# Sixty of 2048 exponential tiles move from ScalarE to VectorE

## The chip, the cores and the metric

The kernel runs on one core of a Trainium2 chip. The core has engines with queues of their own that work at the same time: TensorE (PE, matrix products into PSUM), ScalarE (ACT, functions of one tensor), VectorE (DVE, element by element work), GpSimd (POOL) and SyncE (SP, which starts most DMA transfers here). An engine takes its queue in order; engines wait for each other by semaphores. The metric is device microseconds from start to end of one execution; less is better.

## The reference, cut to what matters

Two branches read the same `x` of 2048 rows and 512 columns. Branch A is attention with 32 heads of 16 dimensions; branch B is a state space convolution. A sigmoid gate mixes them.

```python
q, k, v = heads(x @ wqkv)                    # 32 heads, 2048 rows, 16 columns
p = softmax(einsum("bhqd,bhkd->bhqk", q, k) * 16 ** -0.5)
a = concat(einsum("bhqk,bhkd->bhqd", p, v)) @ wo
K = einsum("dn,dnl,dn->dl", Cc, exp(dt * A * l), dt * Bc).real
b = causal_convolution(x, K) + x * Dskip     # by FFT in the reference
g = sigmoid((x * gate_w).sum(-1))
out = g * a + (1 - g) * b
```

The softmax needs 32 x 2048 x 2048 exponentials. On 128 partitions that is 2048 tiles of 128x512.

## The kernel before, in words

**Tiles.** A block is 512 query rows by four heads, and there are 32 blocks (`NQ` = 512 quads are 32 blocks x 16 key tiles). A quad is four tiles of 128 keys x 512 queries, one for each of the four heads of the block. Four heads lie on the 32-row strips of the array, and a mask (`Qm`, L669) selects which of the two heads in a strip is meant.

**The main loop** (L1366 to L1380) walks over 683 groups of three tiles; the last has two. For each group `qk` (L679) multiplies keys and masked queries into the three PSUM banks of `SC0` or `SC1`, in turn; `ex` (L691) takes the exponential of all three banks in one ScalarE instruction (L693) and writes them in bfloat16 to the ring `ET` of 15 tiles; `pv` (L696) multiplies four tiles with the values (and a column of ones, which sums the softmax's denominator) into the bank `OA`, over the 16 key tiles of a block. After that VectorE moves `OA` out by a transpose (`norm_a`, L707), divides (`norm_b`), and transposes each pair of blocks into `OnT` (`norm_c`). The scores of group g+2 go to the banks of group g, so they wait until those have been read.

**All other work is laid into the gaps.** `Sched` (L239) holds threads: generators that yield an engine, a cost and a priority, and conditions (`AFTER`, `LOCK`). While it records group g, `fill` (L331) takes those threads' next steps that by the planner's estimate fit before ScalarE ends. The order is then fixed: each engine's queue is what this planner wrote at build time. Threads are the projections (`projs`), the parameters, tables and scan of branch B (`params`, `table`, `sstage`, `scan`, `ystage`), the weighted sums (`pvs`), the divisions (`norms`), the masks (`qms`) and the output projection (`outs`, L1218), which adds the gated branches and writes out. Most of these share the one bank `MB`, under a lock, and VectorE moves their results out of it.

**Filling matmuls.** `zeros` (L1358) adds matmuls of a zero tile (`wm`) to `OA`, which change no sum, up to a budget of `FILL` = 1400 columns a group (`want`, L1352). In 5 groups of every 20 (`CYCLE`, `LOWS`, `quiet` at L1349) steps marked low, the small matmuls of `sstage` and `ystage` and those of the gate, are held back, and the budget is 512 columns at a time.

**SBUF** is placed by the first and last group in which a buffer is used (`place`, L473). `Q0` to `Q3` and `OnT0` to `OnT3` hold 2048 columns each.

Every helper records its instruction through one line: matmuls appear as L565, many VectorE products as L721.

Of the kernel before, what the change touches and what calls it, by code (L numbers as in the profile page):

```python
# [25 lines left out]
SGH = 144  # L26
NSG = 2
LATE = 2.0
CYCLE, LOWS = 20, 15
EDGE = 384  # L30
VW = 152


# [205 lines left out]
class Sched:  # L239
# [10 lines left out]
    def add(self, gen, prio):  # L250
        if self.p.cap is not None:
            self.p.cap.append(lambda: self.add(gen, prio))
            return
        t = Thread(gen, prio, self.n)
        self.n += 1
        self.pull(t)
        if t.seg is not None:
            self.thr.append(t)

    def mark(self, name):  # L260
# [17 lines left out]
    def pull(self, t):  # L278
        t.conds, t.seg = [], None
        y = t.nxt  # L280
        if y is None:
            y = next(t.gen, None)
        while y is not None and y[0] in ("AFTER", "LOCK"):
            t.conds.append(y)
            y = next(t.gen, None)
        if y is None:
            assert not t.conds
            return
        t.eng, t.cost = y[0], y[1]
        t.up = y[2] if len(y) > 2 else t.prio  # L290
        t.low = len(y) == 4
        t.end = len(y) == 5
        assert self.p.cap is None
        self.p.cap = []
        t.nxt = next(t.gen, None)
        t.seg, self.p.cap = self.p.cap, None
        if t.nxt is None:
            t.gen = iter(())

    def est(self, t):  # L300
        for c in t.conds:
            if c[0] == "AFTER" and c[1] not in self.flag:
                return None
            if c[0] == "LOCK" and self.lock.get(c[1]) not in (None, t.n):
                return None
        at = self.p.tm[t.eng]
        for a in t.seg:
            if isinstance(a, tuple):
                r = self.p.ready(a)
                if r is None:  # L310
                    if a is t.seg[0]:
                        return None
                    continue
                at = max(at, r)
        return at

    def issue(self, t):
        for c in t.conds:
# [9 lines left out]
        if t.seg is None:  # L328
            self.thr.remove(t)

    def fill(self, until, slack, zeros, lack, quiet=False):  # L331
# [33 lines left out]
class Thread:  # L365

    def __init__(self, gen, prio, n):
        self.gen, self.prio, self.n = gen, prio, n
        self.nxt = None
        self.conds, self.seg, self.eng, self.cost, self.up, self.low, self.end = [], None, None, 0, prio, False, False  # L370


def declare(nc, es):
# [12 lines left out]
    for k in range(4):  # L386
        sb(f"OnT{k}", S)
    sb("OT", 512, FP32)
    sb("ON", 512)
    sb("Rz", 2 * 16, FP32)  # L390
# [6 lines left out]
    sb("hm", 2, FP32)  # L397
    sb("piota", 4, FP32)
    sb("hpi", 1, FP32)

    sb("gwT", 4)
    sb("wm", D)
# [146 lines left out]

def record(nc, p, B, ins):  # L550
    KT, Qm, VE, ET, OT, ON, Rz = (B[n] for n in ("KT", "Qm", "VE", "ET", "OT", "ON", "Rz"))
    OnT = [B[f"OnT{k}"] for k in range(4)]
# [6 lines left out]
    NG = (NSL + 2) // 3  # L559
    x_t, w_t = ins["x"], ins["w"]  # L560
    MM, QUAD, TRI = .23, .34, .33

# [87 lines left out]

    def proj_ev(kind, idx, c, bank):
        b, off, sl = bank
        o, at, ky = (KT, idx * S + 512 * c, (idx, c)) if kind == "K" else (B[f"Q{c}"], 512 * idx, idx)
# [12 lines left out]

    def mk_qm(b):
        qc, pi, w = b // 8, (b % 8) // 2, b % 2
        op("DVE", lambda v: v.tensor_scalar(Qm(512 * (b % 2), [[1, 512]]), B[f"Q{qc}"](512 * pi, [[1, 512]]),  # L669
                                            msk(w, [[1, 1]]), None, ALU.mult), [(B[f"Q{qc}"], pi), (msk, 0)], [(Qm, b % 2, b)], c=.32)  # L670
# [6 lines left out]
    def slots(g):  # L677
        return range(3 * g, min(3 * g + 3, NSL))

    def qk(g):  # L680
        sc = SC[g % 2]
        n = len(slots(g))
        for i, s in enumerate(slots(g)):
            q, j, b, kt, pi = at_slot(s)
            mm(lambda i=i: sc(512 * i, [[1, 512]]),
               lambda j=j, pi=pi, kt=kt: KT(pi * S + 128 * kt, [[1, 128]], 32 * j, 32),
               lambda j=j, b=b: Qm(512 * (b % 2), [[1, 512]], 32 * j, 32),
               [(KT, (pi, kt // 4)), (Qm, b % 2, b)], [(sc, k, g) for k in (range(n) if i == 0 else [i])], pos=(32 * j, 0),
               c=TRI if i == 0 else 0, a=128)

    def ex(g):  # L691
        sc, e, n = SC[g % 2], (3 * g) % NS, len(slots(g))
        op("ACT", lambda a: a.activation(ET(512 * e, [[1, 512 * n]]), sc(0, [[1, 512 * n]]), AF.Exp, scale=DH ** -0.5),  # L693
           [(sc, i, g) for i in range(n)], [(ET, s % NS, s) for s in slots(g)], c=.063 + .4267 * n, lat=.1)

    def pv(q):  # L696
        b, kt = divmod(q, 16)
        pi, w = (b % 8) // 2, b % 2
        for j in range(4):
            hh, e = 2 * j + w, (4 * q + j) % NS  # L700
            mm(lambda j=j: OA(0, [[1, 512]], 32 * j, 32), lambda hh=hh: VE((pi * 16 + kt) * VW + 17 * hh, [[1, 32]]),
               lambda e=e: ET(512 * e, [[1, 512]]),
               [(VE, (pi, kt))] + [(ET, (4 * q + i) % NS, 4 * q + i) for i in (range(4) if j == 0 else [j])],
               [(OA, 0, b)], kt == 0, kt == 15, pos=(0, 32 * j), c=QUAD if j == 0 else 0, a=128)

    def norm_a(b):
# [7 lines left out]

    def norm_c(b):
        qc, pi = b // 8, (b % 8) // 2
        op("DVE", lambda v: v.transpose(OnT[qc](pi * 512, [[1, 512]]), ON(0, [[1, 512]])), [(ON, 0), (ON, 1)],  # L717
           [(OnT[qc], pi)], c=.7)
# [475 lines left out]
    def out_mm(lt, bank, pi, first=0):  # L1194
# [3 lines left out]
        for c2 in range(2):  # L1198
            for h in range(2):
                mm(lambda c2=c2, h=h: b(off + 256 * c2, [[1, 256]], 64 * h, 64),  # L1200
                   lambda c2=c2: OnT[qc](pi * 512 + 128 * r + 64 * c2, [[1, 64]]), lambda h=h: Wo(pi * D + 256 * h, [[1, 256]]),
                   [(OnT[qc], pi), (Wo, 0)], [(b, sl, ('o', lt))], pi == first and c2 == 0, last, pos=(0, 64 * h), c=.14 if h == 0 else 0, a=128)

    def out_ev(lt, bank, o, off, add, at, R, W):
        b, bo, sl = bank
# [32 lines left out]
    def projs():  # L1238
# [21 lines left out]
            sch.mark(f"{kind}{i}.{c}")  # L1260
        sch.mark("projs")

    def pvs():
        for q in range(NQ - 1):
            b, kt = divmod(q, 16)
            if kt == 0 and b >= 1:
                yield ("AFTER", f"n{b - 1}")
            if b < 8 and b % 2 == 0 and kt % 4 == 0:
                yield ("AFTER", f"V{b // 2}.{kt // 4}")
            yield ("PE", QUAD, 0, 0, 0) if kt == 15 else ("PE", QUAD)  # L1270
            pv(q)
            sch.mark(f"pv{q}")
# [52 lines left out]
    proj_ev("K", 0, 0, (SC[0], 0, 0))  # L1325
    qk(0)
    proj_ev("Q", 0, 0, oa)

# [10 lines left out]
        sch.add(th, pr)  # L1339

    def need(g):
        for s in slots(g):
            q, j, b, kt, pi = at_slot(s)
            sch.force(f"K{pi}.{kt // 4}")
            sch.force(f"qm{b}")
# [3 lines left out]
    def quiet():  # L1349
        return p.q % CYCLE >= LOWS  # L1350

    def want():  # L1352
        n = 512 if quiet() else FILL - p.act + lack[0] + (EDGE if sch.kt in (13, 14) else 0)
        if sch.now is None or sch.now == "z" and p.ready((0, ("PE", 0, (), [(OA, 0)]))) > p.tm["ACT"]:
            return 0
        return max(0, min(n, 1024 - lack[1]))

    def zeros():  # L1358
        b, n = sch.now, min(512, want() // 32 * 32)
# [6 lines left out]
    for g in range(NG):  # L1366
        p.q = g
        old = (3 * g + 2 - NS) // 4
        if old >= 0:
            sch.force(f"pv{old}")  # L1370
        ex(g)
        sch.mark(f"g{g}")
        sch.mark(f"blk{at_slot(3 * g)[2]}")
        if g + 1 < NG:
            need(g + 1)
            qk(g + 1)
        t = p.tm["ACT"]
        sch.fill(t, .5, zeros, want, quiet())
        lack[0] = max(min(lack[0] + FILL - p.act, 384), 0)
        p.act = lack[1] = 0  # L1380
    while sch.thr:
        p.q += 1
        sch.fill(1e9, 1e9, lambda: False, lambda: 0)
# [49 lines left out]
```

## Time and profile before

| | before |
|---|---|
| median of 3 runs | 946.11 us (945.63 to 946.46) |
| profiled execution | 945.2 us |
| its span, first to last instruction | 943.4 us |
| ScalarE busy | 924.8 us, of it 917.6 in 683 exponentials (L693) |
| TensorE busy | 790.8 us, of it 240.4 in matmuls of the zero tile |
| VectorE busy | 634.4 us |
| GpSimd busy | 14.6 us |
| mean granted TensorE clock | 0.995 |

The page lists for each engine the time in which at least one of its instructions ran. A row of the groups names the line, the engine, what is written from what, the shape and the count; after the first bar stand the busy time of the group and the mean length of one instruction in ns, after the second the idle time of the engine just before them and what ended it. Instructions of one engine can overlap in time, so a group's busy time can be less than its count times the mean length. Where a mean is longer than the distance from one instruction to the next, the distance is the one that adds up.

### The profile page before, as it was taken

How to read it: one execution, taken by the hardware profiler on the slowest of the kernel's cores; microseconds unless marked ns; L12 is line 12 of the kernel's file. 1: busy time of each engine (PE TensorE's matmuls, PEld its weight loads, DVE VectorE, ACT ScalarE, POOL GpSimd, SP SyncE). 2: the span in 40 equal slices, each digit the busy share in tenths (PEclk: the TensorE clock that was granted, in tenths of full speed). 3: DMA queues.
4: the chain of work that ended last, by engine and by line, in shares of the span. 5: the costliest groups of instructions: out<-in, count | busy, mean ns of one | idle time of the engine just before them, and what ended most of it. 6: DMA issues, size and time to landing. Idle time of an engine off the chain costs nothing.

```text
span 943.4 us, 17746 instructions
## 1 busy us (share of the span) xinstructions
PE 790.8 (84%) x7493; PEld 271.1 (29%) x7606; DVE 634.4 (67%) x1353; ACT 924.8 (98%) x693; POOL 14.6 (2%) x16
## 2 busy tenths in 40 slices
PE   7998888878787777778898888998789899898874
PEld 2333232222222222222333223332233333333221
DVE  5799999997877999999992259942369911113302
ACT  6999999999999999999999999999999999999995
POOL 4000000000000000100000000000000000000000
PEclk9999999999999999999999999999999999999998
DMA  9300000018695566471423562324412222101000
GB/s 190 96 2 1 1 1 1 1 23 197 161 221 159 147 148 148 145 168 29 107 57 80 85 120 80 81 57 90 79 29 77 63 59 71 43 18 39 13 1 23
DMA packets 171472, 73.40 MB, mean 78 GB/s; under 512 B 150272, under 2 KB 159104, under 8 KB 169344
## 3 DMA queue, kind: packets, MB, share of 16 engines
q1 hardware_dynamic: 169088, 71.07, 32.5%
q10 hardware_dynamic: 2304, 1.18, 0.6%
q8 instruction: 60, 0.98, 0.4%
q14 instruction: 20, 0.16, 0.1%
HBM read 30.02 MB, written 25.17 MB: 58 GB/s over the span
## 4 chain that ended last, share of the span: by engine, by line
ACT 96%; PE 1%; DMA 1%; DVE 1%; issue 0%; ACTq 0%; DVEq 0%
ACT ET L693 96%; DMA Wq<-in_A_wqkv_dram 1%; PE OA L565 1%; PE SC L565 0%; PE MB L565 0%; DVE fo L1208 0%; ACTq L569 0%; DVE OT L707 0%; DVE OnT L717 0%; DVE KT L654 0%; ACT e L781 0%; ACT ea L779 0%; DVE ON L712 0%; DVE Rz L711 0%; ACT ge L1185 0%
## 5 line engine op out<-in xcount | busy, mean ns | idle before, releaser
L693 ACT ACTIVATE ET<-SC 128x1536 bf16<-128x1536 f32 (+1 forms) x683 | 917.6, 2021 | 2.7 <-PE SC L565 2.7
L565 PE MATMUL SC<-Qm,KT 32*128 32x512 bf16 x2048 | 267.1, 385 | 113.8 <-ACT ET L693 90.9
L565 PE MATMUL OA<-wm 128*128 128x512 bf16 (+5 forms) x769 | 240.4, 363 | 14.7 <-issue 11.3
L565 PE MATMUL OA<-ET,VE 128*32 128x512 bf16 x2048 | 204.9, 391 | 3.5 <-DVE OT L707 3.0
L565 PEld LDWEIGHTS SC<-Qm,KT 32*128 32x128 bf16 x2048 | 66.4, 91 | 342.6 <-ACT ET L693 331.7
L1009 DVE TENSOR_TENSOR SG<-MB,sgn 128x496 bf16<-128x496 f32 x64 | 43.0, 672 | 74.0 <-PE MB L565 73.8
L565 PEld LDWEIGHTS OA<-ET,VE 128*32 128x32 bf16 x2048 | 52.7, 93 | 126.2 <-issue 116.4
L565 PEld LDWEIGHTS OA<-wm 128*128 128x128 bf16 x870 | 60.5, 97 | 84.5 <-issue 68.4
L707 DVE STREAM_TRANSPOSE OT<-OA 128x512 f32<-128x512 f32 x32 | 22.9, 715 | 70.2 <-PE OA L565 70.2
L1117 DVE TENSOR_TENSOR Yl<-MB,g 128x256 bf16<-128x256 f32 x32 | 13.5, 421 | 77.1 <-PE MB L565 77.0
L721 DVE TENSOR_TENSOR tt<-B,D 128x1024 bf16<-128x1024 bf16 x96 | 62.3, 684 | 0.5
L1042 DVE TENSOR_TENSOR G<-s,s 128x256 f32<-128x256 f32 x120 | 50.7, 423 | 3.4
L565 PE MATMUL MB<-SG,Py 128*64 128x32 bf16 x1024 | 51.0, 230 | 0.0
L1032 DVE TENSOR_TENSOR s<-G,MU 128x256 f32<-128x256 f32 x120 | 50.1, 418 | 0.1
L1038 DVE TENSOR_TENSOR s<-s,SG 128x256 f32<-128x256 f32 x120 | 50.0, 417 | 0.0
L1035 DVE TENSOR_TENSOR s<-G,MU 128x256 f32<-128x256 f32 x120 | 50.0, 417 | 0.0
L565 PEld LDWEIGHTS MB<-SG,Py 128*64 128x64 bf16 x1024 | 30.5, 116 | 28.9 <-issue 28.8
L1045 DVE CAST SG<-G 128x256 bf16<-128x256 f32 x120 | 35.7, 298 | 3.5
L721 DVE TENSOR_TENSOR ft<-FP,L 128x1024 f32<-128x1024 f32 (+1 forms) x32 | 33.9, 1087 | 0.4
L721 DVE TENSOR_TENSOR PT<-tt,tt 128x1024 bf16<-128x1024 bf16 x48 | 32.8, 684 | 0.5
L565 PE MATMUL MB<-XZ,Qt 128*128 128x64 bf16 x512 | 29.5, 195 | 0.0
L1208 DVE SCALAR_TENSOR_TENSOR fo<-MB,g,Yl 128x256 bf16<-128x256 f32 x24 | 11.6, 484 | 25.4 <-PE MB L565 24.9
(129 smaller groups left out, 439.5 us busy)
## 6 DMA issues: line engine op xcount, KB each, us to landing
gm_ptd<-PT SPq DMA_DIRECT2D x16, 1024.0 KB, 5.7
Py<-gm_ptd SPq DMA_DIRECT2D x32, 512.0 KB, 4.1
gm_kpd<-Kst SPq DMA_DIRECT2D x16, 256.0 KB, 4.5
Tt<-gm_kpd SPq DMA_DIRECT2D x128, 32.0 KB, 3.5
gm_xrd<-in_A_x_dram SPq DMA_DIRECT2D x1, 2048.0 KB, 13.1
XS<-gm_xrd SPq DMA_DIRECT2D x8, 256.0 KB, 4.9
XR<-gm_xrd SPq DMA_DIRECT2D x8, 256.0 KB, 5.2
out_dram<-fo SPq DMA_DIRECT2D x28, 64.0 KB, 2.1
```

What stands on the lines that cost most here:

```text
L565: op("PE", lambda t: t.matmul(out(), lhsT(), rhs(), start=start, stop=stop, skip_group_check=True, **kw), R, W, c=c, lat=.15, a=a)
L693: op("ACT", lambda a: a.activation(ET(512 * e, [[1, 512 * n]]), sc(0, [[1, 512 * n]]), AF.Exp, scale=DH ** -0.5), [(sc, i, g) for i in ran ...
L707: op("DVE", lambda v: v.transpose(OT(0, [[1, 512]]), OA(0, [[1, 512]])), [(OA, 0, b)], [(OT, 0, b)], c=.72)
L721: op(eng, lambda v: v.tensor_tensor(o(), a(), b_(), f), R, W, c=c)
L1009: op("DVE", lambda v, bank=bank: v.tensor_tensor(sg(2 * SGH + CB * bl + 8 * bank, [[2 * SGH, 31], [SGH, 2], [1, 8]]), MB(0, [[1, 31], [256 ...
L1032: op(e, lambda v: v.tensor_tensor(s2(0, [[128, 2], [1, 128]]), G(0, [[128, 2], [1, 128]]), MU(d0, [[0, 2], [1, 128]]), ALU.mult), key("G", ...
L1035: op(e, lambda v: v.tensor_tensor(s3(0, [[128, 2], [1, 128]]), G(128, [[-128, 2], [1, 128]]), MU(D + d0, [[D, 2], [1, 128]]), ALU.mult), k ...
L1038: op(e, lambda v, so=so: v.tensor_tensor(s2(0, [[128, 2], [1, 128]]), s2(0, [[128, 2], [1, 128]]), sg(so, [[SGH, 2], [1, 128]]), ALU.add), ...
L1042: op(e, lambda v: v.tensor_tensor(G(0, [[1, 256]]), s2(0, [[1, 256]]), s3(0, [[1, 256]]), ALU.add), [(s2, 0), (s3, 0)], [(G, 0)], c=.38)
L1045: op(e, lambda v, so=so: v.tensor_copy(sg(so, [[SGH, 2], [1, 128]]), G(0, [[128, 2], [1, 128]])), key("G"), ks if c < NCH - 2 else [(sg, ( ...
L1117: op("DVE", lambda v: v.tensor_tensor(Yl(16 * blk + 8 * hf, [[256, 32], [1, 8]]), MB(0, [[1, 32], [32, 8]]), B["g1"](0, [[1, 32], [0, 8]]) ...
L1208: op("DVE", lambda v, c2=c2, c=c: v.scalar_tensor_tensor(o(off + 256 * c2, [[1, 256]]), b(bo + 256 * c2, [[1, 256]]), B["g"](c, [[1, 1]]), ...
```

## The change

The exponentials of 60 tiles, 15 quads of the 512, are computed by VectorE. `compose` forms the groups while the program is recorded: a group has either three tiles for ScalarE, or two for ScalarE and, in its third bank, one for VectorE. `dve_slot` picks a quad ahead of time, not before the last table step of branch B (`K15`) and not while a quarter of the scan is waiting. The number of groups stays 683, of which 61 have two tiles for ScalarE; the last of them had so before.

For such a tile VectorE does five instructions. `exp_in` reads the bank and writes an integer: the score times 2^23 / ln 2 / 4 plus a constant, whose bits taken as a float are a negative power of two times a mantissa (a straight-line stand-in for 2^x). `exp_out` masks the mantissa out (`em`), forms a cubic in it with two multiply-adds (`eu`), and multiplies with the power in a third, into the buffer `ED` of four tiles. The cubic is scaled so that its leading coefficient is one. The exponentials of ScalarE get the same factor: a bias `ln(ESC)`, which is read from the new 128x1 tile `lnc`. The factor cancels in the softmax. All 683 exponentials of ScalarE have this bias; before, the bias was the constant zero in the instruction.

`dpv` multiplies the quad of VectorE with the values, in place of its turn in `pvs`, and the last key tile of the block waits for it. Threads now record a step only when it is chosen (`capture`), since which buffer a quad lies in is known late. The pauses for low steps become 6 groups in 30 (`CYCLE, LOWS = 30, 24`), the budget of zero columns is scaled by the group's length, `Wo` is loaded after group 540 instead of 400, and `Q` and `OnT` become 16 buffers of 512 columns each.

The core of the diff:

```diff
-CYCLE, LOWS = 20, 15
+CYCLE, LOWS = 30, 24
+POLY = (-0.10644581, 0.70747665, -1.37730927, 1.77561576)
+ESC = -1 / (8 * POLY[0])
+EW = 2
...
-    for k in range(4):
-        sb(f"Q{k}", 4 * 512)
+    for k in range(16):
+        sb(f"Q{k}", 512)
+        sb(f"OnT{k}", 512)
...
+    op("DVE", lambda v: v.memset(B["lnc"](0, [[1, 1]]), math.log(ESC)), [], [(B["lnc"], 0)])
...
     def ex(g):
-        sc, e, n = SC[g % 2], (3 * g) % NS, len(slots(g))
-        op("ACT", lambda a: a.activation(ET(512 * e, [[1, 512 * n]]), sc(0, [[1, 512 * n]]), AF.Exp, scale=DH ** -0.5),
-           [(sc, i, g) for i in range(n)], [(ET, s % NS, s) for s in slots(g)], c=.063 + .4267 * n, lat=.1)
+        at, d = GRP[g]
+        sc, e, n = SC[g % 2], RING[at[0]], len(at)
+        op("ACT", lambda a: a.activation(ET(512 * e, [[1, 512 * n]]), sc(0, [[1, 512 * n]]), AF.Exp, scale=DH ** -0.5,
+                                         bias=B["lnc"](0, [[1, 1]])),
+           [(sc, i, g) for i in range(n)] + [(B["lnc"], 0)], [(ET, RING[s], s) for s in at], c=.063 + .4267 * n, lat=.1)
+
+    em, eu, ED = (B[n] for n in ("em", "eu", "ED"))
+    r2, r1, r0 = (POLY[i] / POLY[0] for i in (1, 2, 3))
+    one = [[1, 512]]
+
+    def exp_in(k, g, d):
+        eL, sc, i = B[f"eL{k % EW}"], SC[g % 2], len(GRP[g][0])
+        yield ("DVE", .68, -2)
+        op("DVE", lambda v: v.tensor_scalar(eL.int(0, one), sc(512 * i, one), DH ** -0.5 / math.log(2) * 2 ** 23, 124.0 * 2 ** 23 - 2.0 ** 31,
+                                            ALU.mult, ALU.add), [(sc, i, g)], [(eL, 0, d)], c=.68)
+        sch.mark(f"ei{k}")
+
+    def exp_out(k, d):
+        eL = B[f"eL{k % EW}"]
+        yield ("AFTER", f"ei{k}")
+        if k:
+            yield ("AFTER", f"eo{k - 1}")
+        yield ("DVE", .42, 2.5)
+        op("DVE", lambda v: v.tensor_scalar(em.int(0, one), eL.int(0, one), 0x7fffff, 0x3f800000, ALU.bitwise_and, ALU.bitwise_or),
+           [(eL, 0, d)], key("em"), c=.42)
+        yield ("DVE", .69, 2.5)
+        op("DVE", lambda v: v.scalar_tensor_tensor(eu(0, one), em(0, one), r2, em(0, one), ALU.add, ALU.mult), key("em"), key("eu"), c=.69)
+        yield ("DVE", .69, 2.5)
+        op("DVE", lambda v: v.scalar_tensor_tensor(eu(0, one), eu(0, one), r1, em(0, one), ALU.add, ALU.mult), key("em", "eu"), key("eu"), c=.69)
+        yield ("DVE", .69, 2.5)
+        op("DVE", lambda v: v.scalar_tensor_tensor(ED(512 * (d % 4), one), eu(0, one), r0, eL(0, one), ALU.add, ALU.mult),
+           key("eu") + [(eL, 0, d)], [(ED, d % 4, d)], c=.69)
+        sch.mark(f"eo{k}")
+        sch.mark(f"es{d}")
...
-        yield ("AFTER", "g400")
+        yield ("AFTER", "g540")
...
+    def dpv(q):
+        for j in range(4):
+            yield ("AFTER", f"es{4 * q + j}")
+        yield ("AFTER", f"pv{q // 16 * 16}")
+        yield ("PE", QUAD)
+        pv(q)
+        sch.mark(f"dp{q}")
...
+    def budget():
+        return FILL * (.063 + .4267 * len(GRP[g][0])) / 1.343
+
     def want():
-        n = 512 if quiet() else FILL - p.act + lack[0] + (EDGE if sch.kt in (13, 14) else 0)
+        n = 512 if quiet() else budget() - p.act + lack[0] + (EDGE if sch.kt in (13, 14) else 0)
...
+        if d is not None:
+            sch.add(exp_in(nd, g, d), 1)
+            sch.add(exp_out(nd, d), 1)
+            nd += 1
```

More of the change, by code (lines that the diff above doesn't have):

```diff
@@ L256, in add @@
         self.pull(t)
-        if t.seg is not None:
+        if not t.done:
             self.thr.append(t)
@@ L287, in pull @@
             assert not t.conds
+            t.done = True
             return
@@ L292, in pull, with capture @@
         t.end = len(y) == 5
+    def capture(self, t):
         assert self.p.cap is None
@@ L305, in est @@
                 return None
+        if t.seg is None:
+            self.capture(t)
         at = self.p.tm[t.eng]
@@ L327, in issue @@
         self.pull(t)
-        if t.seg is None:
+        if t.done:
             self.thr.remove(t)
@@ L368, in __init__ @@
         self.gen, self.prio, self.n = gen, prio, n
-        self.nxt = None
+        self.nxt, self.done = None, False
         self.conds, self.seg, self.eng, self.cost, self.up, self.low, self.end = [], None, None, 0, prio, False, False
@@ L385, in declare @@
     sb("ET", NS * 512)
-    for k in range(4):
-        sb(f"OnT{k}", S)
     sb("OT", 512, FP32)
@@ L399, in declare @@
     sb("hpi", 1, FP32)
+    sb("lnc", 1, FP32)
+    for k in range(EW):
+        sb(f"eL{k}", 512, FP32)
+    sb("em", 512, FP32)
+    sb("eu", 512, FP32)
+    sb("ED", 4 * 512)
     sb("gwT", 4)
@@ L551, in record @@
     KT, Qm, VE, ET, OT, ON, Rz = (B[n] for n in ("KT", "Qm", "VE", "ET", "OT", "ON", "Rz"))
-    OnT = [B[f"OnT{k}"] for k in range(4)]
+    OnT = [B[f"OnT{k}"] for k in range(16)]
     OA, MB = B["OA"], B["MB"]
@@ L558, in record @@
     NSL = 4 * NQ
-    NG = (NSL + 2) // 3
+    OFF, GRP, RING, OWN = [], [], {}, {}
     x_t, w_t = ins["x"], ins["w"]
@@ L652, in proj_ev @@
         b, off, sl = bank
-        o, at, ky = (KT, idx * S + 512 * c, (idx, c)) if kind == "K" else (B[f"Q{c}"], 512 * idx, idx)
+        o, at, ky = (KT, idx * S + 512 * c, (idx, c)) if kind == "K" else (B[f"Q{4 * c + idx}"], 0, 0)
         op("DVE", lambda v: v.tensor_copy(o(at, [[1, 512]]), b(off, [[1, 512]])), [(b, sl, ('p', kind, idx, c))],
@@ L668, in mk_qm @@
         qc, pi, w = b // 8, (b % 8) // 2, b % 2
-        op("DVE", lambda v: v.tensor_scalar(Qm(512 * (b % 2), [[1, 512]]), B[f"Q{qc}"](512 * pi, [[1, 512]]),
-                                            msk(w, [[1, 1]]), None, ALU.mult), [(B[f"Q{qc}"], pi), (msk, 0)], [(Qm, b % 2, b)], c=.32)
+        op("DVE", lambda v: v.tensor_scalar(Qm(512 * (b % 2), [[1, 512]]), B[f"Q{4 * qc + pi}"](0, [[1, 512]]),
+                                            msk(w, [[1, 1]]), None, ALU.mult), [(B[f"Q{4 * qc + pi}"], 0), (msk, 0)], [(Qm, b % 2, b)], c=.32)
     def at_slot(s):
@@ L675, in at_slot @@
         return q, j, b, kt, (b % 8) // 2
-    def slots(g):
-        return range(3 * g, min(3 * g + 3, NSL))
     def qk(g):
         sc = SC[g % 2]
-        n = len(slots(g))
-        for i, s in enumerate(slots(g)):
+        at, d = GRP[g]
+        allsl = at + ([] if d is None else [d])
+        n = len(allsl)
+        for i, s in enumerate(allsl):
             q, j, b, kt, pi = at_slot(s)
@@ L691, in ex @@
     def ex(g):
[L692 to L694 removed]
+        at, d = GRP[g]
+        sc, e, n = SC[g % 2], RING[at[0]], len(at)
[28 more added lines that the diff above has]
+        sch.mark(f"es{d}")
     def pv(q):
@@ L699, in pv @@
         for j in range(4):
-            hh, e = 2 * j + w, (4 * q + j) % NS
+            hh = 2 * j + w
+            et, e = (ED, [(ED, i, 4 * q + i) for i in range(4)]) if q in OFF else (ET, [(ET, RING[4 * q + i], 4 * q + i) for i in range(4)])
             mm(lambda j=j: OA(0, [[1, 512]], 32 * j, 32), lambda hh=hh: VE((pi * 16 + kt) * VW + 17 * hh, [[1, 32]]),
-               lambda e=e: ET(512 * e, [[1, 512]]),
-               [(VE, (pi, kt))] + [(ET, (4 * q + i) % NS, 4 * q + i) for i in (range(4) if j == 0 else [j])],
+               lambda et=et, k=e[j][1]: et(512 * k, [[1, 512]]),
+               [(VE, (pi, kt))] + (e if j == 0 else [e[j]]),
                [(OA, 0, b)], kt == 0, kt == 15, pos=(0, 32 * j), c=QUAD if j == 0 else 0, a=128)
@@ L716, in norm_c @@
         qc, pi = b // 8, (b % 8) // 2
-        op("DVE", lambda v: v.transpose(OnT[qc](pi * 512, [[1, 512]]), ON(0, [[1, 512]])), [(ON, 0), (ON, 1)],
-           [(OnT[qc], pi)], c=.7)
+        op("DVE", lambda v: v.transpose(OnT[4 * qc + pi](0, [[1, 512]]), ON(0, [[1, 512]])), [(ON, 0), (ON, 1)],
+           [(OnT[4 * qc + pi], 0)], c=.7)
     def tt(eng, o, a, b_, f, R, W, c):
@@ L1200, in out_mm @@
                 mm(lambda c2=c2, h=h: b(off + 256 * c2, [[1, 256]], 64 * h, 64),
-                   lambda c2=c2: OnT[qc](pi * 512 + 128 * r + 64 * c2, [[1, 64]]), lambda h=h: Wo(pi * D + 256 * h, [[1, 256]]),
-                   [(OnT[qc], pi), (Wo, 0)], [(b, sl, ('o', lt))], pi == first and c2 == 0, last, pos=(0, 64 * h), c=.14 if h == 0 else 0, a=128)
+                   lambda c2=c2: OnT[4 * qc + pi](128 * r + 64 * c2, [[1, 64]]), lambda h=h: Wo(pi * D + 256 * h, [[1, 256]]),
+                   [(OnT[4 * qc + pi], 0), (Wo, 0)], [(b, sl, ('o', lt))], pi == first and c2 == 0, last, pos=(0, 64 * h), c=.14 if h == 0 else 0, a=128)
     def out_ev(lt, bank, o, off, add, at, R, W):
@@ L1261, in projs @@
         sch.mark("projs")
+    def dpv(q):
[5 more added lines that the diff above has]
+        sch.mark(f"dp{q}")
     def pvs():
         for q in range(NQ - 1):
+            if q in OFF:
+                continue
             b, kt = divmod(q, 16)
+            if kt == 15:
+                for k in OFF:
+                    if k // 16 == b:
+                        yield ("AFTER", f"dp{k}")
             if kt == 0 and b >= 1:
@@ L1269, in pvs @@
                 yield ("AFTER", f"V{b // 2}.{kt // 4}")
+            yield ("AFTER", f"cq{q}")
             yield ("PE", QUAD, 0, 0, 0) if kt == 15 else ("PE", QUAD)
@@ L1325, in record @@
     proj_ev("K", 0, 0, (SC[0], 0, 0))
+    GRP.append(([0, 1, 2], None))
     qk(0)
@@ L1341, in need @@
     def need(g):
-        for s in slots(g):
+        for s in GRP[g][0] + ([] if GRP[g][1] is None else [GRP[g][1]]):
             q, j, b, kt, pi = at_slot(s)
@@ L1358, in zeros @@
     def zeros():
-        b, n = sch.now, min(512, want() // 32 * 32)
+        b, n = sch.now, min(512, int(want() // 32) * 32)
         if n < 96:
@@ L1364, in zeros, with dve_slot @@
         return True
-    for g in range(NG):
+    nxt, pos, quads, left, nd = 0, 0, [], [], 0
+    def dve_slot(cur, act):
+        b, kt = divmod(cur // 4, 16)
+        if not left:
+            if "K15" not in sch.flag or any(f"S{4 * r + 3}" in sch.flag and f"scan{r}" not in sch.flag for r in range(4)):
+                return None
+            if quads and f"dp{quads[-1]}" not in sch.flag:
+                return None
+            for bb in (b, b + 1) if kt < 8 else (b + 1,):
+                q = max([16 * bb + k for k in range(9, 15) if 16 * bb + k not in OFF], default=None)
+                if bb < 32 and q is not None and f"qm{bb}" in sch.flag and (bb > b or q // 1 > 16 * b + kt + 4):
+                    quads.append(q)
+                    OFF.append(q)
+                    left.extend(range(4 * q, 4 * q + 4))
+                    sch.add(dpv(q), 0)
+                    break
+            else:
+                return None
+        rush = left[0] // 64 == b and kt >= 9
+        if nd >= EW and f"eo{nd - EW}" not in sch.flag or nd > 1 and f"eo{nd - 2}" not in sch.flag and not rush:
+            return None
+        for s in left:
+            if s % 4 not in [a % 4 for a in act]:
+                left.remove(s)
+                return s
+        return None
@@ new lines, in compose, with take @@
+    def compose():
+        nonlocal nxt, pos, nd
+        if nxt >= NSL:
+            return False
+        def take(n):
+            nonlocal nxt
+            a = []
+            while len(a) < n and nxt < NSL:
+                if nxt // 4 in OFF:
+                    nxt = (nxt // 4 + 1) * 4
+                    continue
+                a.append(nxt)
+                nxt += 1
+            return a
+        keep = nxt
+        act = take(2)
+        d = dve_slot(act[0], act) if len(act) == 2 and len(GRP) > 2 else None
+        if d is None:
+            nxt = keep
+            act = take(3)
+        g = len(GRP)
+        if not act:
+            return False
+        if pos % NS + len(act) > NS:
+            pos += NS - pos % NS
+        for s in act:
+            RING[s] = pos % NS
+            pos += 1
+            if s % 4 == 3:
+                sch.mark(f"cq{s // 4}")
+        GRP.append((act, d))
+        if d is not None:
+            sch.add(exp_in(nd, g, d), 1)
+            sch.add(exp_out(nd, d), 1)
+            nd += 1
+        return True
@@ L1367, in record @@
+    for s in GRP[0][0]:
+        RING[s] = s
+    nxt = pos = 3
+    g = 0
+    while True:
         p.q = g
-        old = (3 * g + 2 - NS) // 4
-        if old >= 0:
-            sch.force(f"pv{old}")
+        for s in GRP[g][0]:
+            if RING[s] in OWN:
+                sch.force(f"pv{OWN[RING[s]] // 4}")
+            OWN[RING[s]] = s
         ex(g)
         sch.mark(f"g{g}")
-        sch.mark(f"blk{at_slot(3 * g)[2]}")
-        if g + 1 < NG:
+        sch.mark(f"blk{at_slot(GRP[g][0][0])[2]}")
+        more = compose()
+        if more:
@@ L1378, in record @@
         sch.fill(t, .5, zeros, want, quiet())
-        lack[0] = max(min(lack[0] + FILL - p.act, 384), 0)
+        lack[0] = max(min(lack[0] + budget() - p.act, 384), 0)
         p.act = lack[1] = 0
+        if not more:
+            break
+        g += 1
+    NG = len(GRP)
     while sch.thr:
```

## The prediction

> **What bounds the kernel now.** I read the page's totals first, then the chain that ended last, then groups by shape, then single instructions in time, and last the busy time of the stretch that changes.
>
> ```profile
> span 943.4 us, 17746 instructions
> PE 790.8 (84%) x7493; PEld 271.1 (29%) x7606; DVE 634.4 (67%) x1353; ACT 924.8 (98%) x693; POOL 14.6 (2%) x16
> PEclk9999999999999999999999999999999999999998
> ACT 96%; PE 1%; DMA 1%; DVE 1%; issue 0%; ACTq 0%; DVEq 0%
> L693 ACT ACTIVATE ET<-SC 128x1536 bf16<-128x1536 f32 (+1 forms) x683 | 917.6, 2021 | 2.7 <-PE SC L565 2.7
> ```
>
> ScalarE is the bound: 683 exponentials hold it 917.6 us, 1.3435 each, and wait 2.7 us in all. One lasts 2.021 us although they are paced at 1.3435, so each begins some 0.68 us before the one ahead of it ends. The clock is full throughout.
>
> The chain of waits, in order of time, gives the same pace:
>
> ```profile
> 190.80 675.76 ACT ET L693 x503
> 874.70 56.53 ACT ET L693 x42
> ```
>
> 675.76 / 503 = 1.3435 us from end to end. The 42 end at 931.23. After them comes the last exponential of all, which has only two tiles:
>
> ```profile
> 929.25 2.90 ACT L693 ACTIVATE ET<-SC 128x1536 bf16<-128x1536 f32 x2
> ```
>
> This timeline row (start, length) holds the last two and ends at 932.15. A two-tile exponential therefore takes 932.15 - 931.23 = 0.92 us, 0.426 less than a three-tile one (before rounding, 0.917). All ScalarE can gain is 60 x 0.426 = 25.6 us.
>
> **The change part by part.**
>
> *Sixty tiles leave ScalarE.* 60 groups shrink from 1.343 to 0.917 us; the number of groups stays 683. -25.6 us, all on the path.
>
> *Every exponential gets a bias read from memory.* All 683 now take their bias from a 128x1 tile (`lnc`) instead of a constant in the instruction. The change's name doesn't speak of this. The rows that bear on it, grouped by shape:
>
> ```profile
> L1315 ACT ACTIVATE sb__101<-bn 128x512 f32<-128x512 f32 x1 | 0.6, 629 | 0.0
> L779 ACT ACTIVATE ea<-an 128x512 f32<-128x512 f32 x1 | 0.6, 621 | 0.0
> L1317 ACT ACTIVATE cb<-ba,hpi 128x512 f32<-128x512 f32 x1 | 0.7, 707 | 0.0
> L1117 DVE TENSOR_TENSOR Yl<-MB,g 128x256 bf16<-128x256 f32 x32 | 13.5, 421 | 77.1 <-PE MB L565 77.0
> ```
>
> `cb` is the only ScalarE instruction with a bias in memory (`hpi`): 0.707 us against 0.629 and 0.621 of the same shape without one, 0.078 to 0.086 more. VectorE shows such a cost too: L1208, with a 128x1 scalar in memory, takes 0.484 where L1117 of the same 256 columns out of PSUM takes 0.421, 0.063 more. Does that time lie on ScalarE's path? Instructions in time:
>
> ```profile
> 8.38 0.63 ACT L1315 ACTIVATE sb__101<-bn 128x512 f32<-128x512 f32 x1
> 8.91 0.71 ACT L1317 ACTIVATE cb<-ba,hpi 128x512 f32<-128x512 f32 x1
> 13.57 1.45 ACT L693 ACTIVATE ET<-SC 128x1536 bf16<-128x1536 f32 x1 [2.66 <-PE SC L565]
> 14.92 0.62 ACT L779 ACTIVATE ea<-an 128x512 f32<-128x512 f32 x1
> 15.44 1.44 ACT L693 ACTIVATE ET<-SC 128x1536 bf16<-128x1536 f32 x1
> 16.77 0.69 ACT L781 ACTIVATE e<-an 128x512 f32<-128x512 f32 x1
> ```
>
> A successor starts 0.10 us before its predecessor ends (14.92 against 15.02, 15.44 against 15.54). `cb` starts at the same distance, 0.10 before `sb__101` ends, so its 0.078 come after its start. If its successor keeps the rule, it begins 0.078 later. An exponential's successor starts 1.33 us after it (15.44 to 16.77), 0.013 sooner than the pace of 1.343, which is slack. Pace with the bias: 1.33 + 0.078 = 1.408, +0.065 on each. Bounds: 0, if the read is wholly hidden behind the predecessor (a gain is excluded, nothing is removed), and 0.086 on top of 1.343. I take 0.065: it is worked out from the only row of this engine, and VectorE's 0.063 lies beside it. 683 x 0.065 = +44.4 us; ends 0 and +58.7.
>
> The Trainium skill, page "ScalarE: Activation LUTs", section "What ACT_TABLE_LOAD costs", speaks against this change: an ACTIVATE takes 186 ns + 0.833 ns a column with immediates, each 128x1 pointer operand adds about 93 ns, and back-to-back ACTIVATEs overlap by about 93 ns. For 512 columns that makes 706 ns with a pointer, and the row above has 707. By the page the sum would be 683 x 0.093 = +63.5 us instead of +44.4, an estimate; the page doesn't say whether the added part is hidden when a successor is already queued, and no row here shows it.
>
> *VectorE computes the sixty tiles.* By the nearest rows: out of PSUM into integers 0.687 (the cast at L654) to 0.751 (L1323, which has a scalar in memory); the mask 0.426 (L759); three multiply-adds 0.691 each (L812, L828). 0.69 + 0.43 + 3 x 0.69 = 3.19 us a tile, 191 us in all. Order of the built program: 24 tiles fall in groups 358 to 497, 36 in 549 to 677. At 1.343 a group these are about 493 to 750 and 750 to 926 us (whole stretches, some groups without a tile). Busy time there before:
>
> ```profile
> core 0: us, PE busy (x) PEld busy (x) DVE busy (x) ACT busy (x) POOL busy (x), PEclk, DMA share, GB/s
> 493.00:750.00 257.00, 222.11 (x2293) 78.95 (x2328) 150.94 (x390) 257.00 (x193) 0.67 (x2) 1.00 0.36 75
> 750.00:926.00 176.00, 152.68 (x1536) 54.69 (x1553) 36.72 (x84) 175.92 (x132) 0.00 (x0) 1.00 0.14 36
> ```
>
> After: 150.9 + 24 x 3.19 = 227.5 us of VectorE in 257 - 24 x 0.426 = 246.8 (92%), and 36.7 + 36 x 3.19 = 151.5 in 160.7 (94%). It fits, which is its cover; were it gone, each further us of VectorE would be one on the path. With the bias at 0.065 the stretches grow by 193 and 132 exponentials x 0.065 to 259.3 and 169.3, and VectorE is at 88 and 89%.
>
> *A new wait.* The scores two groups on write the bank that VectorE reads, so their matmuls wait for its first instruction (`exp_in`). VectorE's queue is in order: `exp_in` may stand behind a transpose of `OA` (L707) or an eviction of `MB` that waits for PE, and behind the stalled matmuls stand the weighted sums and all other work of PE, then the next exponential. Ends: 0, and the whole 0.426 x 60 = 25.6 us. At 88% I take 1.5 us, near the 2.7 us of waits that the row of L693 has, whose scores cross the same buffers.
>
> *What else moves.* Zero matmuls fall from 870 to 785: off the path. Pauses for small matmuls go from 5 groups in 20 to 6 in 30: work on `MB` is spread otherwise, and the chain meets it only around 870 us; nothing. `Q` and `OnT` are cut into smaller buffers with the same instructions: nothing. The load of `Wo` is released at group 540 instead of 400; in SP's queue it now stands behind more loads for the local stage, and its first reader ran at 837 us before, while group 540 ends at about 739: hidden by some 98 us. The added memset of `lnc` is one column at the start, where VectorE waits: nothing.
>
> *Sum* against the profiled execution's own 945.2 us: - 25.6 + 44.4 + 1.5 = 965.5. The median shown is 946.1, 0.9 above it: **966 us**, +2.1%.
>
> **Rivals.**
>
> *The bias read is hidden* (ends faster). For it: 0.68 us of overlap in steady state, long enough to fetch one column. Against it: `cb` started where a successor always starts and still took 0.078 longer. Then VectorE is at 92 to 94% and the new wait is dearer than 1.5; I take 0.05 us for each of 60 tiles, 3, to 0.2 each, 12. 946.1 - 25.6 + 6.5 in the middle = 927, 921 to 935. It decides if less than 25.6 / 683 = 0.037 us of the bias shows in the pace.
>
> *The hand-over eats the gain with a hidden bias.* Each tile loses 0.426 because `exp_in` comes late: 946. For it: the two-tile group gives PE only 0.917 us for scores, sums and zeros, which follow each other by 1.34 (one score triple to the next) at 501.2 to 502.5 us. Against: zero columns are budgeted by the group's length outside the pauses.
>
> *The clock falls.* With a longer pace and 10% fewer zero columns, TensorE is less dense than ever before. For its price: 128x512 matmuls took 0.628 (`OA<-xT,Wq`) in the cold start and 0.384 later. A group's three runs of matmuls would cost about 3 x 0.24 more than warm, of which some 0.4 is slack: 0.3 a group. If a tenth of the groups ran so: 20 us, 986. Against: the clock row is full to the end.
>
> **How the numbers follow.** Bias in the pace 0.57 (around it 954 to 981: a bias of 0.047 to 0.086); hidden bias 0.32; hand-over 0.05; clock 0.06. Predicted is the likeliest, 966. The range must take in the hidden bias: 921 to 984, which leaves out most of the clock case and the best end of the hidden one, about 0.1. The forecast's own range is 954 to 981. This measurement can tell 0.2% from no change: faster 0.35 (the hidden bias and half of the hand-over), same 0.03, slower 0.62.
>
> **What would show it.** Right: 1024-column exponentials 61 times, idle time before the exponentials under 5 us, and their busy time 683 x 1.408 - 25.6 = 936 us. Hidden bias: 892 us, with the chain leaving ScalarE in the stretches of the tiles. Hand-over: rows of scores waiting for `eL`. Clock: fives in its row. Most likely to be wrong: that a cost seen once, in an instruction whose successor was a table load, is paid in a full queue.

## The result and the profile after

The changed kernel takes 987.9 us (median of 4 runs, 984.7 to 997.9); the kernel before took 945.9 beside it. The ratio is 1.046, with a 95% interval of 1.039 to 1.054. The forecast was 966 us, with 954 to 981 around it and 921 to 984 in all: the direction was right, and the time lies above the whole range.

The profiled execution took 984.7 us. The page of the changed kernel has these lines (totals, clock, chain, exponentials):

```profile
span 982.9 us, 17954 instructions
PE 791.3 (81%) x7409; PEld 269.6 (27%) x7521; DVE 811.3 (83%) x1654; ACT 960.6 (98%) x693; POOL 14.6 (1%) x16
PEclk7999999988999989989999779999999999999998
ACT 93%; PE 4%; DMA 1%; DVE 1%; issue 0%; ACTq 0%; DVEq 0%
L707 ACT ACTIVATE ET<-SC,lnc 128x1536 bf16<-128x1536 f32 (+1 forms) x683 | 953.4, 1832 | 6.1 <-PE SC L578 5.6
```

ScalarE is still the bound, at 98%. Its 683 exponentials now hold it 953.4 us where they held it 917.6, although 60 of them are shorter. Their waits are 6.1 us instead of 2.7. Two things are new: the busy time itself, and a clock row that is no longer full (mean 0.959).

The first instructions of ScalarE in time (start, length) show where the busy time comes from:

```profile
9.31 0.70 ACT L1377 ACTIVATE cb<-ba,hpi 128x512 f32<-128x512 f32 x1
14.68 1.54 ACT L707 ACTIVATE ET<-SC,lnc 128x1536 bf16<-128x1536 f32 x1 [3.38 <-PE SC L578]
16.12 0.62 ACT L824 ACTIVATE ea<-an 128x512 f32<-128x512 f32 x1
16.64 1.53 ACT L707 ACTIVATE ET<-SC,lnc 128x1536 bf16<-128x1536 f32 x1
18.06 0.67 ACT L826 ACTIVATE e<-an 128x512 f32<-128x512 f32 x1
```

An exponential lasts 1.54 us where it lasted 1.45, and its successor still starts 0.10 before its end: 14.68 to 16.12 is 1.44, and 16.64 to 18.06 is 1.42 where the kernel before had 1.33. The chain of waits gives the pace over a longer piece, and shows how it breaks off:

```profile
18.73 178.87 ACT ET L707 x125
197.72 18.61 ACT ET L707 x13
216.70 0.61 PE SC L578 x3
217.31 1.08 PE OA L578 x4
218.39 0.54 PE SC L578 x3
```

178.87 / 125 = 1.431 us, against 1.3435 before: +0.0875 for each exponential. From 216.7 on the chain runs over TensorE: three score matmuls that took 0.32 to 0.39 in the chain of before (at 866 to 874 us) now take 0.54 to 0.61. The busy time by stretch tells why; this answer's columns are those shown with the prediction, the clock is the number after POOL:

```profile
213.00:228.00 15.00, 13.86 (x66) 2.74 (x68) 13.34 (x20) 14.36 (x11) 0.34 (x1) 0.54 0.04 18
551.60:568.60 17.00, 15.94 (x127) 5.09 (x127) 11.95 (x21) 15.63 (x12) 0.00 (x0) 0.50 0.39 78
```

In these stretches TensorE runs at half clock, is busy for 92 to 94% of the time, and holds ScalarE up, which is busy for 14.36 of 15 us and 15.63 of 17. Added up over the trace, exponentials end 4.5 us later than at a pace of 1.431 (1.0045 for two tiles), 3.8 of it in ten exponentials in or just behind such stretches.

The waits are hardly those of VectorE's tiles. Of the 6.1 us, 3.38 stand before the first exponential (the row above; 2.66 in the kernel before), and the rest in or just behind the half-clock stretches, 1.3 of it at 556 to 562 us, where the first of these tiles lie too. From 568.8 us on, with 52 of the 60 tiles still to come, ScalarE's timeline is one row without a wait:

```profile
568.82 402.85 ACT L707 ACTIVATE ET<-SC,lnc 128x1536 bf16<-128x1536 f32 x297
```

### The profile page after: what moved, and what is told of

It reads as the page before. It is cut to its first block, busy times and chain, and to the rows that moved or that the text cites. A ratio compares the mean times of both kernels' runs of the same rounds, so it can differ in the third digit from the quotient of the medians.

```text
span 982.9 us, 17954 instructions
## 1 busy us (share of the span) xinstructions
PE 791.3 (81%) x7409; PEld 269.6 (27%) x7521; DVE 811.3 (83%) x1654; ACT 960.6 (98%) x693; POOL 14.6 (1%) x16
## 4 chain that ended last, share of the span: by engine, by line
ACT 93%; PE 4%; DMA 1%; DVE 1%; issue 0%; ACTq 0%; DVEq 0%
ACT ET L707 93%; PE OA L578 2%; PE SC L578 2%; DMA Wq<-in_A_wqkv_dram 1%; PE MB L578 0%; DVE fo L1253 0%; ACTq L582 0%; DVE OT L752 0%; DVE OnT L762 0%; DVE KT L668 0%; ACT e L826 0%; ACT ea L824 0%; DVE ON L757 0%; DVE Rz L756 0%; ACT ge L1230 0%
## 5 line engine op out<-in xcount | busy, mean ns | idle before, releaser
L707 ACT ACTIVATE ET<-SC,lnc 128x1536 bf16<-128x1536 f32 (+1 forms) x683 | 953.4, 1832 | 6.1 <-PE SC L578 5.6
L578 PE MATMUL SC<-Qm,KT 32*128 32x512 bf16 x2048 | 276.4, 398 | 158.7 <-ACT ET L707 146.0
L578 PE MATMUL OA<-wm 128*128 128x512 bf16 (+9 forms) x684 | 223.3, 374 | 15.4 <-issue 12.8
L578 PEld LDWEIGHTS OA<-wm 128*128 128x128 bf16 x785 | 55.7, 98 | 86.9 <-issue 73.3
L718 DVE TENSOR_SCALAR eL<-SC 128x512 int32<-128x512 f32 x60 | 41.2, 688 | 38.3 <-PE SC L578 38.0
L735 DVE SCALAR_TENSOR_TENSOR ED<-eu,eL 128x512 bf16<-128x512 f32 x60 | 41.4, 689 | 1.3
L733 DVE SCALAR_TENSOR_TENSOR eu<-eu,em 128x512 f32<-128x512 f32 x60 | 41.3, 688 | 1.4
L731 DVE SCALAR_TENSOR_TENSOR eu<-em 128x512 f32<-128x512 f32 x60 | 41.1, 686 | 0.9
```

The lines of the kernel that those rows point to most:

```text
L578: op("PE", lambda t: t.matmul(out(), lhsT(), rhs(), start=start, stop=stop, skip_group_check=True, **kw), R, W, c=c, lat=.15, a=a)
L718: op("DVE", lambda v: v.tensor_scalar(eL.int(0, one), sc(512 * i, one), DH ** -0.5 / math.log(2) * 2 ** 23, 124.0 * 2 ** 23 - 2.0 ** 31, A ...
L731: op("DVE", lambda v: v.scalar_tensor_tensor(eu(0, one), em(0, one), r2, em(0, one), ALU.add, ALU.mult), key("em"), key("eu"), c=.69)
L733: op("DVE", lambda v: v.scalar_tensor_tensor(eu(0, one), eu(0, one), r1, em(0, one), ALU.add, ALU.mult), key("em", "eu"), key("eu"), c=.69)
L735: op("DVE", lambda v: v.scalar_tensor_tensor(ED(512 * (d % 4), one), eu(0, one), r0, eL(0, one), ALU.add, ALU.mult), key("eu") + [(eL, 0, ...
```

## The experiments

The diffs are cut to what differs; where `lnc` is added to the kernel before, its declaration and its memset come with it.

**One: the bias alone taken back.** The queues of all engines keep their order; only the operand differs, and the cubic's factor is taken off in VectorE's integer constant.

```diff
-AF.Exp, scale=DH ** -0.5, bias=B["lnc"](0, [[1, 1]])),
+AF.Exp, scale=DH ** -0.5),
...
-DH ** -0.5 / math.log(2) * 2 ** 23, 124.0 * 2 ** 23 - 2.0 ** 31,
+DH ** -0.5 / math.log(2) * 2 ** 23, (124.0 - math.log2(ESC)) * 2 ** 23 - 2.0 ** 31,
```

> The changed kernel, every queue in the same order, but the exponentials of ScalarE have the constant zero as bias again; the factor of the cubic is taken off in the integer constant of VectorE instead (minus log2(ESC) in the exponent). Theory one, the bias read from memory is the whole loss: the pace of three-tile exponentials returns from 1.431 to 1.343 us, 61 two-tile ones at 0.917, so 946 - 25.6 = 920.5 and a few us of waits of ScalarE on scores, 921 to 930. Rival, VectorE's load and its new wait make the loss: the pace stays above 1.40 or the idle time before the exponentials rises to 20 us and more, and the time stays at or above 946. Rival, the clock: it stays near 0.95 here too, since the zero columns are the same, and costs about 5 us.

Measured: 922.8 us (921.5 to 923.0), ratio 0.976 (0.974 to 0.977) to the kernel before. The same instructions, one operand apart, are 65 us faster than the changed kernel. Its groups by shape:

```profile
L707 ACT ACTIVATE ET<-SC 128x1536 bf16<-128x1536 f32 x622 | 849.5, 1857 | 4.6 <-PE SC L578 4.4
L707 ACT ACTIVATE ET<-SC 128x1024 bf16<-128x1024 f32 x61 | 72.1, 1266 | 0.0
```

Two lines of its page, totals and clock:

```profile
PE 771.5 (84%) x7409; PEld 266.6 (29%) x7521; DVE 806.3 (88%) x1654; ACT 900.2 (98%) x693; POOL 14.6 (2%) x16
PEclk9999999999899899999999999999999999999998
```

The same groups of the changed kernel:

```profile
L707 ACT ACTIVATE ET<-SC,lnc 128x1536 bf16<-128x1536 f32 x622 | 907.7, 1875 | 5.9 <-PE SC L578 5.4
L707 ACT ACTIVATE ET<-SC,lnc 128x1024 bf16<-128x1024 f32 x61 | 79.3, 1398 | 0.2 <-PE SC L578 0.2
```

907.7 - 849.5 is 58.2 us over 622, 0.094 each, with what the half-clock stretches add to the busy time. VectorE carries the same sixty tiles at 88% of a shorter span, and ScalarE waits 4.6 us, 2.0 of it before the first exponential and 0.7 in the stretch of the tiles (497 to 902 us). So VectorE's share and its new wait are not what made the change slower; they bring 22.6 us (945.4 - 922.8) of the 25.6 that sixty tiles are worth. The rival that put the loss on the hand-over falls.

**Two: the bias alone put into the kernel before.**

```diff
-AF.Exp, scale=DH ** -0.5),
+AF.Exp, scale=DH ** -0.5, bias=B["lnc"](0, [[1, 1]])),
```

> The kernel before, with the one difference that all 683 exponentials read their bias (ln of ESC) from a 128x1 tile; all tiles on ScalarE, pauses as before. Theory one: +0.088 us on each of 683, +60 us, 1006 (1000 to 1010), and the granted clock falls below 0.99 if the longer pace is what thins TensorE's work. Rival, the loss comes from VectorE's part: 946 to 950. Rival of the forecast, a front end at 1.408: +44, 990.

Measured: 1009.6 us (1008.1 to 1012.5), ratio 1.068 (1.066 to 1.070), +64.2 us, at a clock of 0.954 to 0.969. The bias costs this without any tile on VectorE. It is more than 60, and the clock is lower, so a second cost seems to come with it; experiment four separates the two. A front end at 1.408 us, which the forecast had taken, is refuted: it would have given 990.

**Three and four: more zero columns.** The changed kernel, and the kernel of experiment two, with a budget that is longer by the ratio of the paces.

```diff
-FILL = 1400
+FILL = 1492
```

> The changed kernel with FILL = 1492 instead of 1400, which is 1400 x 1.431 / 1.343: as many budgeted columns of matmul for each us as the kernel before had. If the thinner work of TensorE is what lets the clock fall, the clock returns to 0.99 and the time falls by the 5 us of long exponentials that lie in the half clock stretches, to 979 to 981, with a narrower spread than 984 to 998. If the clock falls for another reason (pauses 6 in 30), it stays near 0.95 and so does the time, 984 to 998.

> The kernel before with the bias from memory and FILL = 1492. Theory one: the pace is still 1.431, since no clock of TensorE bounds it, so 1005 to 1007, with the clock at 0.99. If the clock rather than the bias read made part of the longer pace, this is clearly faster than the same kernel without more zeros.

Measured: the changed kernel 983.3 us (980.1 to 988.5), at clocks of 0.963 to 0.991; the single runs go with their clock (980.1 at 0.991, 981.9 at 0.983, 984.7 at 0.975, 988.5 at 0.963). The kernel before with the memory bias 1004.4 us (1003.3 to 1007.1) at 0.986 to 0.991, 5.2 less than without the zeros and 59.0 above the kernel before. Its clock row:

```profile
PEclk9999999999999999999999999999999999999998
```

and two pieces of its chain of waits, in order of time:

```profile
17.82 187.45 ACT ET L696 x131
205.39 786.82 ACT ET L696 x550
```

The clock row is full again and the chain stays with ScalarE, at 187.45 / 131 = 1.431. The pace is therefore the same at a full clock; 59.0 us are the bias, and the clock adds some 5 here. In the changed kernel the spread reaches beyond the expected 979 to 981: more zeros help there, but not in every run; the one at a clock of 0.991 took 980.1.

**Five: every other exponential.** The kernel before, with a bias of zero; the 341 exponentials of odd groups read it from memory.

```diff
+bias=B["lnc"](0, [[1, 1]]) if g % 2 else 0.0),
```

> The kernel before, with a bias of zero that only the 341 exponentials of odd groups read from a 128x1 tile. Theory one, each instruction that reads its bias pays 0.088 us by itself, whatever its value and its neighbours: 341 x 0.088 = +30 us, 975 (973 to 978). Rival, the price is paid at the start of an instruction (starts 1.330 us apart without, 1.423 with) and the run-ahead of the plain ones absorbs a part: mean of starts 1.3765 against the pace of 1.3435, 683 x 0.033 = +22.5, 968. Rival, it is paid only where two in a row read a bias: 946 to 948.

Measured: 974.7 us (973.2 to 976.5), +29.1, ratio 1.030 (1.028 to 1.033), at 0.983 to 0.992. ScalarE in time, from this kernel:

```profile
41.51 1.60 ACT L696 ACTIVATE ET<-SC 128x1536 bf16<-128x1536 f32 x1
42.84 1.70 ACT L696 ACTIVATE ET<-SC,lnc 128x1536 bf16<-128x1536 f32 x1
44.26 1.62 ACT L696 ACTIVATE ET<-SC 128x1536 bf16<-128x1536 f32 x1
45.59 1.72 ACT L696 ACTIVATE ET<-SC,lnc 128x1536 bf16<-128x1536 f32 x1
```

After a plain one the next starts 1.33 us later, after one with `lnc` 1.42, from the start (the medians over the run are 1.330 and 1.425). In ends: 43.11 to 44.54 is 1.43, 44.54 to 45.88 is 1.34. The instruction that reads the bias pays for it alone, and the run-ahead of the plain one takes nothing off: both rivals (968, and 946 to 948) fall. The value of the bias plays no part, since a bias of zero costs the same. Nor is it the new dependency on `lnc`, which is declared for all exponentials here, the plain ones too.

**Six and seven: the pauses.** The kernel of experiment one with the old pauses, and the kernel before with the new ones.

```diff
-CYCLE, LOWS = 30, 24
+CYCLE, LOWS = 20, 15
```

> The changed kernel with the constant bias, and CYCLE, LOWS = 20, 15 as before. With the new pauses and the constant bias it took 922.8 us at a clock of 0.986. If the fewer pauses lower the clock, the clock rises to 0.993 and the time falls by some 1 to 2 us, to about 921; if the pauses buy the gaps that VectorE's tiles need, fewer tiles or more waits show and the time rises to 924 to 935.

> The kernel before with the new pauses alone, CYCLE, LOWS = 30, 24; no tiles on VectorE, constant bias. The forecast held them for nothing: 945 to 946. If they thin the clock, as one could ask of the 0.959 of the changed kernel, the clock falls below 0.98 and the time rises to 948 to 952.

Measured: 930.8 us (929.4 to 931.9) at 0.984 to 0.989, 8.0 more than with the new pauses; and 947.1 us (945.5 to 950.8) for the new pauses alone, ratio 1.0018 (1.0002 to 1.0033), at clocks of 0.984 to 0.994, between the two times that were expected. The new pauses hardly lower the clock: alone to a mean of 0.989, against 0.992 for the kernel before beside it, and the old ones don't raise it in the shorter kernel. For the first of the two kernels the time was as expected (924 to 935), but not the reason: the tiles are again sixty, and ScalarE ends within 1.0 us of where it ended with the new pauses. VectorE in time, after the last exponential (908.7 us) of the kernel with the old pauses:

```profile
908.01 1.00 DVE L1252 SCALAR_TENSOR_TENSOR fo<-MB,g,Yl 128x256 bf16<-128x256 f32 x2 [4.13 <-PE MB L578]
910.32 1.00 DVE L1252 SCALAR_TENSOR_TENSOR fp<-MB,g,Yl 128x256 f32<-128x256 f32 x2 [1.31 <-PE MB L578]
...
918.10 1.00 DVE L1252 SCALAR_TENSOR_TENSOR fp<-MB,g,Yl 128x256 f32<-128x256 f32 x2 [1.59 <-PE MB L578]
919.02 0.71 DVE L751 STREAM_TRANSPOSE OT<-OA 128x512 f32<-128x512 f32 x1
```

and with the new ones, where the last exponential ends at 909.7:

```profile
910.25 0.72 DVE L751 STREAM_TRANSPOSE OT<-OA 128x512 f32<-128x512 f32 x1 [4.74 <-PE OA L578]
```

With the old pauses the output projection through `MB` isn't done when the exponentials are; the last transpose starts at 919.0 instead of 910.3. The pauses hold back the small matmuls that go before it. Those of `ystage` (`MB<-SG,Py`: shortest, median and longest in ns, then first and last start), with the old pauses and with the new:

```profile
L578 PE MATMUL MB<-SG,Py x1024: 222/232/245, 431.4 to 859.6; 128*64 128x32 bf16 x171
L578 PE MATMUL MB<-SG,Py x1024: 223/233/243, 434.1 to 820.2; 128*64 128x32 bf16 x171
```

The last of them starts 39 us later with the old pauses. In the shorter kernel fewer pauses are worth 8 us, at the end.

**Eight: experiment one with more zeros.** `FILL` goes from 1400 to 1470, nothing else.

> The changed kernel with the constant bias and FILL = 1470. In the run with FILL = 1400 the clock fell to a half at 233 to 240 and 308 to 315 us and exponentials there took up to 2.35 us, some 3 us over their pace in all. If 5% more zero columns hold the clock, it is 0.99 and the time 919.5 to 921; if they cost TensorE more than they bring (it has 0.917 us for a two-tile group), waits of ScalarE on scores rise and the time is 923 to 930.

Measured: 920.4 us (919.9 to 922.4), ratio 0.973 (0.971 to 0.975), at 0.987 to 0.994: the lowest median here, 25 us below the kernel before, and within the expected 919.5 to 921. The 2.4 us to experiment one aren't clear of the spread: the two ranges overlap.

## Why the prediction was right and wrong

**The bound and the mechanism** were right; the size of one term was not, nor was the clock, which the sum had at nothing. The chain stayed with ScalarE (93%), and the operand that the change's name doesn't mention decides the sign: +65 us with it, experiment one against the changed kernel, and -22.6 without. Of the signs named, the 61 two-tile exponentials came; the exponentials' busy time was 953.4 us instead of 936, and the idle time before them 6.1 instead of under 5.

**Sixty tiles leave ScalarE, -25.6 us.** Right: the kernels with the constant bias have 61 two-tile exponentials, 60 more than before, and the two that keep the new pauses are faster by 22.6 and 25.2 us.

**Every exponential gets a bias from memory, +44.4 us.** This is the term that was mis-sized, by two choices in one step. First, 0.078 us was read from the single `cb`; the same read costs 0.093 in an exponential (starts 1.423 apart instead of 1.330). Second, 0.013 was taken off because successors start 1.33 apart while the pace is 1.343. That is no slack: with the bias the ends are again further apart than the starts (1.431 and 1.423), so the pace rose by 0.0875, of which the forecast had 0.065. 683 x 0.0875 = 59.8, and experiment four measured 59.0 with the clock held. The upper bound, 0.086 or 58.7 us, was just too low. The Trainium skill's figure, page "ScalarE: Activation LUTs", section "What ACT_TABLE_LOAD costs", is 93 ns for a pointer operand; the distance of starts agrees to the nanosecond, the pace (0.0875) lies a little under it. The measurement decides. 683 x 0.093 = 63.5 in the sum would have given 985, nearer to the 987.9, but in part by luck: what it has above 59.8 covers some of the clock's cost.

With 59.8 in place of 44.4 the forecast's sum gives 981, still within its range. What carried the time beyond 984 was the clock, which the sum had at nothing.

**The hidden read** (0.32) fell: nothing is hidden, with 0.4 us of run-ahead in the queue (one lasts 1.832 at a pace of 1.431). The run-ahead was the reason for this rival, and experiment five shows that it has no part in the price.

**VectorE's sixty tiles.** Right within 1%: the five rows by which they were priced gave 3.19 us, the measured ones are 0.688, 0.419, 0.686, 0.688 and 0.689, 3.17 in all, and VectorE was busy for 811.3 us against 634.4 + 191 in the forecast. The 14 us less are overlap of neighbours: the lengths of all its instructions add up to 699.4 us before and 890.2 after, 190.8 more. **The new wait** was taken at 1.5 us at the slower pace. ScalarE's waits rose by 3.4 in the changed kernel, but 0.7 of that is before the first exponential and the rest lies at half clock; after 568.8 us, with 52 of the 60 tiles still to come, none shows. In experiment one, at the fast pace, 0.7 us lie in the stretch of the tiles, where 3 to 12 had been set. The hand-over as a loss (0.05) fell.

**The clock** was a rival of its own with 0.06, and its price 20 us. It isn't a rival: it comes with the forecast's own longer pace. A longer pace with the same or fewer columns thins TensorE's work, which the text said, and then set aside since the row of before is full, although that row belongs to the shorter pace. Columns of matmul that the program gives TensorE (by its own budget count, in which a matmul on one of four strips counts 128; zeros included) for each measured us, and the clocks of the runs:

| kernel | columns per us | granted clock |
|---|---|---|
| constant bias, more zeros | 1222 | 0.987 to 0.994 |
| constant bias, old pauses | 1207 | 0.984 to 0.989 |
| before | 1205 | 0.988 to 0.997 |
| constant bias | 1191 | 0.984 to 0.990 |
| before, new pauses | 1185 | 0.984 to 0.994 |
| memory bias, every other | 1169 | 0.983 to 0.992 |
| memory bias in before, more zeros | 1164 | 0.986 to 0.991 |
| changed, more zeros | 1153 | 0.963 to 0.991 |
| memory bias in before | 1129 | 0.954 to 0.969 |
| changed | 1113 | 0.916 to 0.959 |

The clocks are means over the whole span, so they hold its end too: with the old pauses the 21 us after the last exponential run at 0.55. All kernels at 1164 columns and more stay at 0.983 or above; the three at 1153 and less have runs at 0.969 or below. That this mean decides isn't shown: the time it is divided by is itself longer when the clock falls, and the constant bias has stretches at half clock too, at 1191 (the eights in its clock row). What experiments three and four show is that more zero columns, at the same pace, raise the clock. Nor does the profile show long gaps: in the changed kernel's trace none between two matmuls is longer than 1.04 us from 30 to 970 us.

The clock cost 5.2 us by experiment four. In the changed kernel, 945.9 + 59.8 - 25.6 = 980.1 is an estimate for a full clock, and experiment three's run at 0.991 took just that. 987.9 were measured, so some 8 us in the median are the clock's, with the waits that come with it.

**Pauses at nothing.** Alone they cost 1.5 us (947.1 against 945.7), near nothing. But their cover, that the work on `MB` has time to spare, is gone when the exponentials end 25 us sooner: there the old pauses cost 8 us. In the slower changed kernel this was not tried.

## What to carry to other kernels

Count a cost per instruction by all instructions that get it: one operand that turns from a constant into a 128x1 tile cost 0.0875 us, and on 683 paced instructions it outweighed a gain of 25.6 us; folding the constant into another step gave the gain back. A price seen once in an isolated instruction may be paid in a full queue as well, and a distance of starts shorter than that of ends isn't slack until a run shows it. When the bounding engine slows, ask what becomes of the filling work, more of which brought TensorE's clock back here, and when it speeds up, what is left to do after its last instruction.

## What was not expected of the hardware

The price of the read is paid by the instruction that reads and by no neighbour (1.43 and 1.34 from end to end in turn), although in these rows each starts some 0.27 us before the one ahead of it ends (42.84 against 43.11). And the clock answers to a few per cent: from 1205 to 1129 columns per us, 6% less, it went from 0.99 to between 0.954 and 0.969, and at 1164, 3% more, it was back at 0.986 to 0.991.
